# A build-time time model lets its DMAs land half a microsecond later

## The chip, the cores and the metric

The kernel runs on one core of one Trainium2 chip. The metric is the device time of one execution in microseconds (us). One first execution of 3502.34 us enters no ratio. Times of the same kernel differ a little from chip to chip.

## The reference

It is one adaLN transformer block: 2048 tokens of width 512, 32 heads of width 16, and a gated FFN of width 1792, all in bf16.

```python
mod = (_silu(c) @ w_mod)                      # six vectors of 512: sa, ca, ga, sb, cb, gb
h = _layernorm(x) * (1 + ca) + sa
x = x + ga * (softmax(q @ k.T / 4) @ v) @ wo  # q, k, v = heads of h @ wqkv
h = _layernorm(x) * (1 + cb) + sb
x = x + gb * (_gelu(h @ w_gate) * (h @ w_up)) @ w_down
```

The 32 x 2048 x 2048 exponentials set the pace: ScalarE computes most of them.

## The kernel before

The kernel is a program that writes a program. While it is built, a greedy loop decides at each step what each engine gets next. It asks a time model when an instruction's inputs will be there, and issues nothing that the model holds for not ready. The order that comes out is fixed. On the chip each engine follows its own order, and semaphores hold an instruction until its inputs really are there. So the model's error has a price: if it believes that data land earlier than they do, an engine stands still in front of an instruction with other work queued behind it.

The model of a DMA, in nanoseconds, with the constants it uses:

```python
LAND = 800
RATE = 175
...
    def model(self, op, t, cost):
        eng = op.eng
        if op.stream not in COMPUTE:
            self.free[eng] = t + 460
            early = t < 20000                       # the prologue
            self.dma_free = max(t + 1400, self.dma_free) + cost / (350 if early else RATE)
            op.t1 = self.dma_free + (1500 if early else LAND)
```

The DMAs shown here are those after each unit of attention (8 head groups for each set of query columns; 38 units pass here). Their denominators travel through DRAM, so that the reciprocal is taken 128 partitions wide and then comes back as a broadcast; the second of two units also moves the first one's neighbour rows inside `osb`:

```python
self.copy("dve", osb, acc[:, 0:W])                     # unit_end
self.dma("sp", s1..., self.osb[DH:P:32, lo:hi], "da")  # scr_den <- osb
# ... then as tasks, each issued when the model says its input is there:
self.dma("sp", den, s1..., "db")                       # den <- scr_den
self.recip(rden, den)                                  # VectorE
self.dma("sp", s2..., rden, "dc")                      # scr_rec <- rden
rd(j)    # j = 0..3:  rb <- scr_rec, broadcast to 16 partitions
move(j)  # j = 0..3, second unit only:  osb <- osb, from one 16 partitions to the next
fin2     # onorm <- osb * rb                           # VectorE; the output projection needs it
```

The other part is the "quads". Where the loop finds VectorE free enough by the model, it takes four 512-column score tiles away from ScalarE and computes their exponentials by integer arithmetic on VectorE and GpSimd.

The softmax here doesn't subtract the row's maximum and nothing guards it: scores larger than these inputs give would overflow.

Of the kernel before, what the change touches and what calls it, by code (L numbers as in the profile page):

```python
# [45 lines left out]
NS = 4  # L46
AHEAD = 20
PREFER = 300
LAND = 800
RATE = 175  # L50
POW = (350, 145)
SPACE = 12
# [54 lines left out]
class _Recorder:  # L107
# [181 lines left out]
# [4 lines that stand above are left out]
            early = t < 20000  # L293
            self.dma_free = max(t + 1400, self.dma_free) + cost / (350 if early else RATE)
            op.t1 = self.dma_free + (1500 if early else LAND)
        elif eng == "pe":
# [1456 lines left out]
```

## Time and profile before

| | before |
|---|---|
| median time | 813.48 us (the earlier three runs: 814.04) |
| span of the profiled run | 812.1 us |
| ScalarE busy | 775.7 us |
| ScalarE idle from 25 us to its last exponential | 7.24 us |
| from there to the end ("the tail") | 25.75 us |
| quads | 106 |
| VectorE's waits for den and rb | 9.5 us |

To read it: the last exponential is where ScalarE next loads another activation table (786.35 us here). Two stretches of the table of stretches, cut at that point, give the next two rows. Their columns are first and last us, length, then busy time (instructions) of PE (TensorE), PEld (its weight loads), DVE (VectorE), ACT (ScalarE) and POOL (GpSimd), the granted TensorE clock, the DMA share and GB/s:

```profile
25.00:786.35 761.35, 713.59 (x11725) 243.58 (x11724) 650.80 (x1161) 754.11 (x696) 244.33 (x139) 1.00 0.14 37
786.35:812.10 25.75, 21.85 (x284) 16.90 (x284) 12.11 (x24) 7.13 (x13) 0.80 (x2) 1.00 0.04 11
```

The idle time is 761.35 - 754.11 = 7.24 us. The quads are counted as the prediction does it, and the waits are its rows of rden for den and onorm for rb (8.1 + 1.4).

### The profile page before, as it was taken

To read this page: it belongs to the slowest core of one execution; us is meant where nothing else is said; L and a number is where in the kernel's file an instruction comes from. 1 tells how busy PE (TensorE), PEld (TensorE's weight loads), DVE (VectorE), ACT (ScalarE), POOL (GpSimd) and SP (SyncE) were. 2 spreads that over 40 slices of the span, in tenths; PEclk is the share of its full clock that TensorE was granted. 3 is DMA by queue.
4 is the path that set the end of the run, shared out by engine and by line. 5 is a ranking of instruction groups with operands and counts; after the bars stand their busy time and mean duration, and the time that the engine had idled before them with its cause. 6 is when DMAs were issued, how large, how long until landed. Compare 5 with 4: busy or idle time off the path is not lost.

```text
span 812.1 us, 27576 instructions
## 1 busy us (share of the span) xinstructions
PE 755.9 (93%) x12330; PEld 269.8 (33%) x12330; DVE 680.5 (84%) x1236; ACT 775.7 (96%) x729; POOL 252.4 (31%) x157
## 2 busy tenths in 40 slices
PE   8999999999989899899999998989989899998998
PEld 3333332322222222222222222222434333445466
DVE  6878988987898989898889899988688885697673
ACT  4999999999999999999999999999999899998972
POOL 2101426354465153346335351456130000010020
PEclk9999999999999999999999999999999999999999
DMA  9100000000022121111113111211232221120000
GB/s 313 52 9 12 15 10 15 10 17 10 16 64 62 31 53 48 35 41 29 29 37 94 30 47 45 61 29 29 54 91 57 58 68 39 36 71 11 17 14 14
DMA packets 58616, 36.03 MB, mean 44 GB/s; under 512 B 17961, under 2 KB 55074, under 8 KB 58498
## 3 DMA queue, kind: packets, MB, share of 16 engines
q1 hardware_dynamic: 56114, 32.71, 14.5%
q8 instruction: 96, 1.57, 0.8%
q10 hardware_dynamic: 2384, 1.57, 0.7%
q14 instruction: 22, 0.18, 0.1%
HBM read 29.62 MB, written 2.61 MB: 40 GB/s over the span
## 4 chain that ended last, share of the span: by engine, by line
ACT 69%; PE 19%; DVE 7%; DMA 3%; SPq 1%; issue 1%; POOL 0%; POOLq 0%; DVEq 0%
ACT E L379 66%; PE ps_mi L366 8%; PE ps_sc L366 7%; PE ps_pv L366 4%; ACT wreg L379 2%; DVE mreg L391 1%; DMA den<-scr_den 1%; SPq L430 1%; DVE wreg L400 1%; DMA mreg<-in_w_mod_dram 1%; DVE wreg L396 1%; DVE dreg L391 1%; DVE wreg L383 1%; DVE osb L400 0%; DMA scr_rec<-rden 0%
## 5 line engine op out<-in xcount | busy, mean ns | idle before, releaser
L379 ACT ACTIVATE E<-ps_sc 128x1024 bf16<-128x1024 f32 (+1 forms) x682 | 746.7, 1279 | 19.1 <-PE ps_sc L366 17.5
L391 POOL TENSOR_SCALAR mreg<-dreg 128x2048 uint16<-128x2048 uint16 x92 | 173.1, 1897 | 271.3 <-DVE mreg L391 130.8
L391 DVE TENSOR_SCALAR dreg<-ps_sc 128x512 uint16<-128x512 f32 x247 | 168.1, 687 | 36.1 <-PE ps_sc L366 34.9
L366 PE MATMUL ps_sc<-qT,kme 32*128 32x512 bf16 (+2 forms) x1318 | 172.9, 332 | 12.2 <-ACT E L379 10.2
L366 PE MATMUL ps_sc<-qT,kmo 32*128 32x512 bf16 (+2 forms) x1301 | 170.1, 332 | 6.7 <-ACT E L379 5.3
L366 PE MATMUL ps_pv<-E,vaug 128*17 128x512 bf16 (+2 forms) x2112 | 148.9, 328 | 1.0 <-DVE vaug L400 0.8
L366 PE MATMUL ps_pv<-mreg,vaug 128*17 128x512 bf16 (+2 forms) x1712 | 123.8, 339 | 1.8 <-DVE mreg L391 0.8
L366 PE MATMUL ps_mi<-wreg,mreg 128*32 128x512 bf16 (+1 forms) x1280 | 91.9, 374 | 7.5 <-DVE wreg L400 3.5
L391 POOL TENSOR_SCALAR mreg<-mreg 128x2048 uint16<-128x2048 uint16 x34 | 64.1, 1898 | 106.7 <-DVE mreg L391 57.2
L391 DVE TENSOR_SCALAR mreg<-ps_sc 128x512 uint16<-128x512 f32 x122 | 82.5, 686 | 11.1 <-PE ps_sc L366 9.9
L366 PEld LDWEIGHTS ps_sc<-qT,kme 32*128 32x128 bf16 x1318 | 46.1, 91 | 135.5 <-ACT E L379 108.0
L366 PEld LDWEIGHTS ps_sc<-qT,kmo 32*128 32x128 bf16 x1301 | 44.8, 91 | 127.6 <-ACT E L379 97.5
L391 DVE TENSOR_SCALAR mreg<-dreg 128x2048 uint16<-128x2048 uint16 x118 | 78.7, 686 | 1.5 <-PE ps_pv L366 1.4
L366 PEld LDWEIGHTS ps_pv<-E,vaug 128*17 128x17 bf16 x2112 | 44.0, 89 | 58.5 <-issue 47.3
L366 PEld LDWEIGHTS ps_pv<-mreg,vaug 128*17 128x17 bf16 x1712 | 38.3, 89 | 43.6 <-issue 18.1
L391 DVE TENSOR_SCALAR mreg<-mreg 128x2048 uint16<-128x2048 uint16 x74 | 49.1, 687 | 2.2 <-PE ps_pv L366 2.1
L643 POOL TENSOR_SCALAR mv<-mv 128x4 f32<-128x4 f32 (+2 forms) x10 | 2.3, 231 | 137.0 <-DVE mv L423 129.1
L366 PEld LDWEIGHTS ps_mi<-wreg,mreg 128*32 128x32 bf16 x1280 | 26.5, 95 | 46.4 <-issue 18.4
L366 PE MATMUL ps_mi<-hreg,wreg 128*32 128x512 bf16 x480 | 40.2, 384 | 0.2
L366 PE MATMUL ps_sc<-xs,ident 128*32 128x512 bf16 (+1 forms) x349 | 28.0, 388 | 13.2 <-ACT E L379 12.4
L400 DVE CAST wreg<-ps_mi 128x512 bf16<-128x512 f32 x49 | 33.6, 686 | 6.9 <-PE ps_mi L366 6.4
L396 DVE SCALAR_TENSOR_TENSOR wreg<-wreg,ps_mi 128x512 bf16<-128x512 bf16 x49 | 33.4, 682 | 5.8 <-PE ps_mi L366 3.8
(151 smaller groups left out, 704.8 us busy)
## 6 DMA issues: line engine op xcount, KB each, us to landing
mreg<-in_B_w_up_dram SPq DMA_DIRECT2D x22, 256.0 KB, 3.0
mreg<-in_B_w_gate_dram SPq DMA_DIRECT2D x15, 256.0 KB, 2.9
rb<-scr_rec SPq DMA_DIRECT2D x96, 32.0 KB, 1.8
dreg<-in_B_w_down_dram SPq DMA_DIRECT2D x9, 256.0 KB, 2.8
mreg<-in_w_mod_dram SPq DMA_DIRECT2D x1, 2048.0 KB, 14.6
mreg<-in_B_w_down_dram SPq DMA_DIRECT2D x8, 256.0 KB, 2.7
out_dram<-xs SPq DMA_DIRECT2D x16, 128.0 KB, 1.8
osb<-osb SPq DMA_DIRECT2D x48, 32.0 KB, 1.9
```

The costliest lines, as they stand in the source:

```text
L366: return self.rec("pe", lambda e: e.matmul(out, lhsT, rhs, start=start, stop=stop, tile_position=tp), [lhsT, rhs], [out], cost=(n, int(rhs ...
L379: return self.rec("act", lambda e: e.activation(out, in_, func, scale=scale, **kw), rd, wr, cost=self.cost("act", out, [in_], "act"))
L383: return self.rec(eng, lambda e: e.tensor_tensor(out, a, b, op), [a, b], [out], cost=self.cost(eng, out, [a, b], "tt"))
L391: return self.rec(eng, lambda e: e.tensor_scalar(out, a, s1, s2, **kw), rd, [out], cost=self.cost(eng, out, [a], "ts"))
L396: return self.rec("dve", lambda e: e.scalar_tensor_tensor(out, a, s, b, op0=op0, op1=op1), rd, [out], cost=self.cost("dve", out, [a, b], " ...
L400: return self.rec(eng, lambda e: e.tensor_copy(out, in_), [in_], [out], cost=self.cost(eng, out, [in_], "ts"))
L430: return e.dma_start(out, in_)
L643: self.rec("pool", lambda e: e.tensor_scalar(v, v, EPS, None, op0=ALU.add), [v], [v], cost=200)
```

## The change

```diff
-LAND = 800
+LAND = 1300
```

Nothing else. The model's landing outside the prologue moves by 500 ns, with the intent that readers of DMA'd data stand further back in their engines' order, behind work that can be done meanwhile.

## The prediction

> **What bounds the kernel now.** I read the page first (busy time, slices, chain that ended last), then the waits, the table of stretches, and the timeline of DVE and of the DMA queue around the longest DMA waits.
>
> ```profile
> PE 755.9 (93%) x12330; PEld 269.8 (33%) x12330; DVE 680.5 (84%) x1236; ACT 775.7 (96%) x729; POOL 252.4 (31%) x157
> ...
> ACT  4999999999999999999999999999999899998972
> ...
> ACT 69%; PE 19%; DVE 7%; DMA 3%; SPq 1%; issue 1%; POOL 0%; POOLq 0%; DVEq 0%
> ```
>
> ScalarE (ACT), which computes the exponentials, is busy for 775.7 of 812.1 us and carries 69% of the chain. Its idle time is 36.4 us. The table of stretches (first to last us, length, then busy time and count of PE, PEld, DVE, ACT, POOL, clock, DMA share, GB/s) says where:
>
> ```profile
> 0.00:25.00 25.00, 20.43 (x326) 9.33 (x330) 17.54 (x52) 14.45 (x21) 7.27 (x16) 0.93 0.90 295
> ...
> 300.00:400.00 100.00, 93.60 (x1224) 26.04 (x1220) 89.34 (x148) 100.00 (x96) 40.92 (x23) 1.00 0.14 37
> ...
> 600.00:640.00 40.00, 35.48 (x677) 13.84 (x680) 33.24 (x64) 37.68 (x33) 7.03 (x5) 0.96 0.24 66
> ...
> 720.00:760.00 40.00, 35.78 (x854) 18.63 (x850) 31.86 (x68) 37.27 (x36) 5.66 (x3) 0.96 0.06 12
> ...
> 785.00:812.00 27.00, 22.54 (x306) 17.23 (x302) 13.07 (x27) 8.47 (x15) 0.80 (x2) 1.00 0.03 11
> ```
>
> The start loses 25.0 - 14.45 = 10.55 us and the tail 27.0 - 8.47 = 18.53 us. Everything between, 25 to 785 us, loses 36.4 - 29.1 = 7.3 us, nearly all after 600 (2.3 in 600 to 640, 2.7 in 720 to 760). From 100 to 600 us ACT is full.
>
> ACT's work is not fixed. DVE and POOL take some score tiles ("quads" of four 512-column tiles) by an approximation. The groups give 247 + 122 + 33 + 22 = 424 tiles read from PSUM by DVE at L391, so 106 quads; the shifts agree (92 + 34 on POOL, 118 + 74 on DVE: 318 = 3 x 106). ACT has the rest: 276 activations of three tiles (395.5 us) and 398 of two (391.1 us), 1624 tiles, 786.6 / 1624 = 0.484 us a tile. **One quad more or fewer is worth 4 x 0.484 = 1.94 us of ACT.**
>
> Who waits for DMAs, apart from the DMA queue itself, in the waits (total us, times, longest):
>
> ```profile
> DVE rden L403 <- DMA den<-scr_den: 8.1, 10, 2.2
> ...
> DVE onorm L383 <- DMA rb<-scr_rec: 1.4, 1, 1.4
> ```
>
> After the prologue that is all that matters: no wait of a matmul for a weight load stands among the large ones. DVE's waits are the reciprocal of the softmax denominators and one normalisation. The worst one in the timeline, of DVE and then of the queue that issues the DMAs (SPq):
>
> ```profile
> 737.34 0.42 DVE L383 TENSOR_TENSOR wreg<-wreg 128x512 bf16<-128x512 bf16 x1
> 739.95 0.20 DVE L403 RECIPROCAL rden<-den 128x8 f32<-128x8 f32 x1 [2.19 <-DMA den<-scr_den]
> ...
> 732.98 0.54 SPq L430 DMA_DIRECT2D scr_den<-osb  x1
> 733.57 3.24 SPq L430 DMA_DIRECT2D osb<-osb  x4
> 736.85 0.58 SPq L430 DMA_DIRECT2D den<-scr_den  x1
> 740.18 0.34 SPq L430 DMA_DIRECT2D scr_rec<-rden  x1
> 741.61 1.71 SPq L430 DMA_DIRECT2D rb<-scr_rec  x4
> ```
>
> The path is scr_den, den, reciprocal, scr_rec, rb. Here four moves of osb stood between the first two hops, and from the first issue to the reciprocal 6.97 us went by.
>
> **What the Trainium skill says.** "DMA: Bandwidth & Descriptors", section "Rules for kernel authors", advises to issue a DMA early, compute, and wait late: that is what the change asks of the order. Its section "Two DMAs through the same engine are not ordered" says that a DMA that reads what another wrote must wait for its semaphore, so each hop of the path pays a whole latency; the trace agrees: the DMA queue waits 34.6 us for scr_rec and 16.8 us for scr_den. Its section "Anatomy of one DMA" (for the path issued by GpSimd) gives about 2.0 us fixed; this trace, on SP's path, has medians of 1.8 us to landing for the 8 KB den loads and 2.9 us for 256 KB of weights. "Perfetto Trace Analysis", section "DMA Instruction — HWDGE (DVE, Sync)", says that the reported window ends when the sequencer is free and leaves the data's movement out; agreed: den's row is 0.58 us, its reader starts 3.10 us after the row begins.
>
> **The change, part by part.** It removes and adds no instruction by itself. LAND is a constant of the model by which the program orders its own instructions while it is built; on the chip the semaphores decide. After 20 us of model time a DMA lands at issue + 1400 ns + bytes / 175 + LAND. An 8 KB hop: 1400 + 47 + 800 = 2.25 us, after the change 2.75. 256 KB: 1400 + 1498 + 800 = 3.70 us, after 4.20. Both were already above the medians of 1.8 and 2.9 us; only hops behind other DMAs are slower (3.1 us above, up to 3.9).
>
> (a) Reciprocals. Two hops lie before each of the 38, so it stands about 1.0 us further back. The model's first two hops become 5.5 us instead of 4.5, against 6.97 in the worst case. Of the ten waits (0.3, 0.8, 0.3, 1.1, 0.6, four making 2.8, and 2.2 us) about 1.0 each goes: some 6.5 of the 8.1 us. The onorm wait of 1.4 us, four hops back (2.0 us), goes too. But DVE is not the bound: only what reached ACT counts. Near 485 us ACT lost at most 0.6 us in its whole 100 us; near 670 us none; at 741.7 ACT idled 1.72 us for a DVE product that followed the 2.19 us wait; at 637 to 638 us it idled 1.82 + 0.50 us for scores soon after the onorm wait at 632. The upper end is 0.6 + 1.7 + 1.4 = 3.7 us; I count half, **-1.8 us**.
>
> (b) Later normalisations. A unit of attention (38 of them) is normalised four hops after its end, so 2.0 us later in the model. The output projection and all of the FFN of the set follow it. Before 600 us this is slack: units end about every 20 us, the buffers come free some 11 to 13 us after an end. At the two places where the side work is tight, after the sets that end near 600 and near 730 us, and at the last normalisation (778.2 us, needed by the projection at 780.96, so 2 us of slack), part of 2 us comes back each time. An estimate of half: 3 x 1 x 0.5 = **+1.5 us**.
>
> (c) Weights. Streamed pieces are double buffered, reader and load some 8 us apart in the paced stretch, so 0.5 us is hidden; **0**.
>
> (d) The order as a whole. Every decision is greedy and depends on model times, so it all changes from the first DMA after 20 us on. What decides is how many quads are started. A later model landing makes side work look idle for longer (then quads are allowed freely: more), and moves normalisations back into the time in which DVE takes quads (fewer). I cannot derive the sign. 2 quads either way are 3.9 us; tail alignment is a few us more. The constants look tuned around 800, so I add **+1.8 us** for a disturbed optimum; that is a judgement and no measurement.
>
> Sum: 814.0 - 1.8 + 1.5 + 0 + 1.8 = **815.5 us**.
>
> **The rivals.**
> 1. The model was too optimistic where moves crowd the queue, the waits go, and the time falls by the 3.7 us of (a) or, with more quads, by more: 806 to 811 us. For it: ten waits at the same reciprocal, 6.97 us real against 4.5 modelled. Against: ACT is full for 500 us and idles only 7.3 us between start and tail, so without more quads even a perfect order stays above 806.
> 2. The landing was already pessimistic (1.8 and 2.9 us against 2.25 and 3.70), so readers that were ready stand behind others, side work starts later and the tail grows: each set's 2 us comes through, the side work piles up at the end where PE's ps_mi products lead the chain, and two or three quads are lost: 820 to 828 us. For it: after 600 us the chain is mostly PE and DVE side work. Against: 18.5 us of tail hold no DMA that anything but the end waits for.
> 3. Nothing: ACT's full stretch hides all of it and the two effects cancel, 812 to 816 us.
>
> **Range and chances.** Rival 3 and the middle of 1 and 2 give 806 to 826 us for 8 in 10. A gain of 2% is 16.3 us: more than twice all of ACT's idle time outside start and tail, so it needs at least five quads more as well. A loss of 2% needs eight quads fewer, or a stall of the side work that the buffers cannot hide. Chances: faster 0.03, within 2% 0.90, slower 0.07.
>
> **What would show it.** Step (a) is right if the wait of rden for den falls from 8.1 to about 1.6 us, and the onorm wait goes. Step (b) is right if the onorm rows stand about 2 us later after their unit's osb copy. Step (c): no new wait of PE for wreg, mreg or dreg weight loads. Step (d): the count of L391 reads of PSUM (424) stays within 8; the ACT busy time moves by 1.94 us per quad; ACT's idle time from 25 to 785 us stays below 12 us. The prediction is wrong if the number of quads moves by five or more, or the tail after the last exponential, now 26 us, changes by more than 3 us.

## The result, and the profile after

The changed kernel took 809.41 us in the median of four runs (808.04 to 810.54) against 813.48 for the kernel before. The ratio is 0.9952 with a 95% interval of 0.9928 to 0.9977: half a per cent faster, and within 2%. A ratio here is the mean time of one kernel's runs over that of the other's runs of the same rounds, so not quite the ratio of the quoted medians.

From the page of the changed kernel: busy times, ScalarE's slices, and the chain that ended last.

```profile
PE 752.7 (93%) x12355; PEld 273.1 (34%) x12359; DVE 689.0 (85%) x1252; ACT 770.0 (95%) x733; POOL 262.3 (32%) x162
...
ACT  4999999999999999999999999999999999999961
...
ACT 83%; PE 12%; DVE 3%; DMA 2%; issue 0%; SPq 0%; DVEq 0%
```

ScalarE does 5.7 us less work, carries 83% of the chain in place of 69%, and runs empty earlier (the last two slices are 6 and 1 tenths instead of 7 and 2). The waits for DMAs in the trace of the changed kernel (total us, times, longest):

```profile
DVE onorm L383 <- DMA rb<-scr_rec: 1.4, 1, 1.4
DVE rden L403 <- DMA den<-scr_den: 1.4, 1, 1.4
```

The reciprocals waited 8.1 us before and wait 1.4 us now. The same cut of stretches (the last exponential is over at 777.03 us):

```profile
25.00:777.03 752.03, 707.41 (x11705) 245.07 (x11705) 658.26 (x1176) 749.16 (x702) 254.54 (x145) 1.00 0.14 38
777.03:808.20 31.17, 25.29 (x347) 19.23 (x340) 14.03 (x29) 7.12 (x13) 0.80 (x2) 0.93 0.04 14
```

| us of the span | before | after | difference |
|---|---|---|---|
| ScalarE idle, 25 us to last exponential | 7.24 | 2.87 | -4.37 |
| ScalarE busy in the same stretch | 754.11 | 749.16 | -4.95 |
| tail | 25.75 | 31.17 | +5.42 |
| span (the three rows and the first 25 us) | 812.1 | 808.2 | -3.90 |

The groups count 258 + 134 + 30 + 14 = 436 tiles by integer arithmetic, so 109 quads, three more: 3 x 1.94 = 5.8 us of ScalarE. But the tail took back 5.42 us, in part through the granted clock: its mean was 0.93 there, and 0.50 from 784 to 786 us. From the busy times and clocks of the stretches between 782 and 788 us, an estimate is that 1.4 us of TensorE's 25.29 come from this. So two stories fit the sum: the stalls went and the quads were given back, or the quads were the gain and something else grew the tail. The experiments decide between them.

### The profile page after: what moved, and what is told of

Same layout as the page of the kernel before. It is cut to its first block, busy times and chain, and to the rows that moved or that the text cites. A ratio compares the mean times of both kernels' runs of the same rounds, so it can differ in the third digit from the quotient of the medians.

```text
span 808.2 us, 27649 instructions
## 1 busy us (share of the span) xinstructions
PE 752.7 (93%) x12355; PEld 273.1 (34%) x12359; DVE 689.0 (85%) x1252; ACT 770.0 (95%) x733; POOL 262.3 (32%) x162
## 4 chain that ended last, share of the span: by engine, by line
ACT 83%; PE 12%; DVE 3%; DMA 2%; issue 0%; SPq 0%; DVEq 0%
ACT E L379 80%; PE ps_sc L366 6%; PE ps_mi L366 3%; ACT wreg L379 3%; PE ps_pv L366 2%; DMA mreg<-in_w_mod_dram 1%; DVE mreg L391 1%; DMA den<-scr_den 1%; DMA rb<-scr_rec 0%; DVE wreg L383 0%; DVE dreg L391 0%; SPq L430 0%; DVE wreg L391 0%; DVE xs L383 0%; PE ps_sc L370 0%
## 5 line engine op out<-in xcount | busy, mean ns | idle before, releaser
L379 ACT ACTIVATE E<-ps_sc 128x1024 bf16<-128x1024 f32 (+2 forms) x686 | 742.5, 1265 | 15.6 <-PE ps_sc L366 14.5
L391 POOL TENSOR_SCALAR mreg<-dreg 128x2048 uint16<-128x2048 uint16 x93 | 175.2, 1898 | 271.1 <-DVE mreg L391 114.0
L391 DVE TENSOR_SCALAR dreg<-ps_sc 128x512 uint16<-128x512 f32 x258 | 175.0, 687 | 32.0 <-PE ps_sc L366 30.2
L366 PE MATMUL ps_sc<-qT,kmo 32*128 32x512 bf16 (+2 forms) x1316 | 173.5, 332 | 10.7 <-ACT E L379 9.6
L391 DVE TENSOR_SCALAR mreg<-ps_sc 128x512 uint16<-128x512 f32 x134 | 91.1, 686 | 15.3 <-PE ps_sc L366 14.8
L391 POOL TENSOR_SCALAR mreg<-mreg 128x2048 uint16<-128x2048 uint16 x38 | 71.6, 1898 | 96.1 <-PE ps_sc L366 48.7
L391 DVE TENSOR_SCALAR mreg<-dreg 128x2048 uint16<-128x2048 uint16 x123 | 81.2, 687 | 0.5 <-PE ps_pv L366 0.4
L366 PEld LDWEIGHTS ps_pv<-mreg,vaug 128*17 128x17 bf16 x1768 | 40.4, 89 | 35.0 <-issue 10.9
L366 PE MATMUL ps_sc<-xs,ident 128*32 128x512 bf16 x353 | 28.7, 398 | 11.4 <-ACT E L379 11.2
```

The source lines that it names most:

```text
L366: return self.rec("pe", lambda e: e.matmul(out, lhsT, rhs, start=start, stop=stop, tile_position=tp), [lhsT, rhs], [out], cost=(n, int(rhs ...
L379: return self.rec("act", lambda e: e.activation(out, in_, func, scale=scale, **kw), rd, wr, cost=self.cost("act", out, [in_], "act"))
L391: return self.rec(eng, lambda e: e.tensor_scalar(out, a, s1, s2, **kw), rd, [out], cost=self.cost(eng, out, [a], "ts"))
```

## The experiments

**Theory W:** the loss was the waits for DMAs, and the gain is that they went. **Rival Q:** the gain is the other greedy order with its three more quads; the waits were hidden by a full ScalarE. For the tail, **theory G** (the extra quads' gain is given back there) stands against **rival H** (the quads are the gain).

Where an order is kept and single instructions are moved, the order of the greedy pass was taken as a list, edited, and all dependences and semaphores were worked out anew. With an empty edit this gave the unchanged program. "Modelled end" is the end of the kernel's own time model after the build; with 800 and with 1300 it is the same, 798.2 and 798.1 us. So the model, which believes its own landings, sees no gain in the changed order.

One question needed no run. With 1300 for the five kinds of denominator DMA alone (da, db, dc, dd and the moves) the build gave the changed program, instruction for instruction. With 1300 for all others but these, only the order of a few DMAs on the issuing queue changed. So the whole effect of the change comes through the denominators.

### First group: moving the readers, and the opposite constant

In `rec_later` and `both_later` the readers are moved inside the order of before, in `both_sooner` inside the order of after (a move stops early where a dependence forbids it):

```diff
+ for i in reciprocals(order):     later(order, i, 1000)    # rec_later: 1000 ns of modelled VectorE work
+ for i in normalisations(order):  later(order, i, 1000)    # both_later: these first, then the reciprocals
+ ...                              sooner(order, i, 1000)   # both_sooner
```

`land600` sets the constant the other way:

```diff
-LAND = 800
+LAND = 600
```

> The order of the kernel before is kept, quads and all (106), and only the 38 reciprocals of the denominators are moved behind about 1.0 us more of DVE work each, with the DMAs that depend on them. Theory W (the waits for the DMAs were the loss, made larger by the TensorE clock that drops after the stall): the wait of the reciprocals for den falls from 8.1 us to under 2.5, the stall at 738 to 746 us with its granted clock of 0.50 is gone, ACT's idle time before the last exponential falls by about 2 us, time about 811.5. Theory Q (the gain is the three more quads and another greedy order, the waits were hidden): the wait falls all the same, but the time stays within 1 us of before, 813 to 814.

> As the run with the reciprocals moved, and the 19 normalisations that read the reciprocals' broadcast are moved back by about 1.0 us of DVE work too, as far as their readers allow. Theory W: the stall at 632 to 640 us (onorm for rb, 1.4 us, then granted clock 0.50) goes as well, ACT's idle time before the last exponential falls from 17.8 to about 14 us, time about 810, with 106 quads. Theory Q: 813 to 814.

> The order of the kernel after the change is kept, with its 109 quads, and the reciprocals and normalisations are moved forward by about 1.0 us of DVE work, which gives the waits back. Theory W: the wait of rden for den rises from 1.4 to about 8 us or more, one or two stalls with a low granted clock come back before the last exponential, and the time rises by 2 to 5 us over the kernel after, to 811 to 814. Theory Q: the waits rise and the time stays at 809 to 810.

> The constant is set to 600 instead of 800: the opposite direction. The program that comes out has 109 quads, three more than before, as the changed kernel has, but its readers stand nearer to their DMAs. Theory W: the reciprocals wait longer than 8.1 us, about 15, and most of the gain of the quads (5.8 us of ACT) is lost to stalls: no better than 811. Theory Q: as fast as the changed kernel or faster, 805 to 810.

(The 17.8 us of ScalarE's idle time that `both_later` names count the first 25 us too: 10.55 + 7.24. The tables below leave the start out.)

Measured, against 814.6 us for the kernel before on the same chip:

| run | quads | waits for den + rb, us | ScalarE idle to last exp. | tail | median us | ratio (95%) |
|---|---|---|---|---|---|---|
| rec_later | 106 | 1.0 + 11.8 | 7.70 | 25.94 | 817.33 | 1.0039 (1.0016 to 1.0062) |
| both_later | 106 | 1.3 + 1.1 | 7.81 | 25.76 | 812.63 | 0.9975 (0.9952 to 0.9997) |
| both_sooner | 109 | 14.6 + 3.1 | 11.89 | 31.78 | 821.74 | 1.0109 (1.0079 to 1.0140) |
| land600 | 109 | 11.7 + 3.6 | 8.30 | 27.10 | 811.95 | 0.9974 (0.9956 to 0.9992) |

`rec_later` is a miss of theory W as it was put, and of the 813 to 814 us of rival Q as well: the wait for den went, but the time rose. The waits of its VectorE show what happened to the wait.

```profile
DVE onorm L383 <- DMA rb<-scr_rec: 11.8, 9, 3.7
DVE rden L403 <- DMA den<-scr_den: 1.0, 1, 1.0
```

A later reciprocal starts the next two hops later, and the normalisations at their end had not been moved. The wait went one reader down the path and grew. What this cost is not shown: the profiled run is the fastest of the six (813.62 us against a median of 817.33), and its span, 811.9 us, is that of before.

`both_later` gains a quarter per cent, half of what was expected, although both waits are nearly gone. Its profiled run, the slowest of its six (813.92 us), shows a new stall that the edit made itself: a moved normalisation stood in front of the projection that TensorE needed next, and waited for its own later DMA. The rows of VectorE, of TensorE and of the table of stretches around it:

```profile
593.86 0.69 DVE L383 TENSOR_TENSOR onorm<-osb,rb 128x512 bf16<-128x512 f32 x1 [1.13 <-DMA rb<-scr_rec]
...
594.61 0.62 PE L366 MATMUL ps_mi<-wo,onorm 128*32 128x512 bf16 x4 [2.65 <-DVE onorm L383]
...
594.00:596.00 2.00, 1.39 (x18) 0.41 (x18) 1.27 (x3) 0.00 (x0) 0.00 (x0) 0.50 0.64 176
596.00:598.00 2.00, 2.00 (x25) 0.55 (x26) 1.36 (x3) 1.76 (x2) 0.00 (x0) 0.50 0.33 91
```

This shows what a wait can do. VectorE waits 1.13 us, TensorE behind it is idle for 2.65 us, then the granted clock is 0.50 (in all the stretches from 594 to 600 us), and ScalarE loses 3.8 us for want of scores. Readers pushed back by hand, with the rest left where it is, are no clean test; the greedy pass plans around them and this edit does not.

`both_sooner` is the opposite: the changed order, 109 quads, with the readers moved forward. The waits come back (17.7 us) and the time is 1.1% above before, more than the 811 to 814 us that were expected. `land600` has the same number of quads as the changed kernel and a modelled end of 793.8 us, the best of all, but 15.3 us of waits; it gains a quarter per cent where theory Q expected 805 to 810 us. Both speak for W, but both change more than the waits.

### Second group: the readers stay, the DMAs land sooner

The clean test leaves the order of the four compute engines alone and takes away what delays the landing. The prediction's timeline shows four moves of 16 partitions inside `osb` between the first two hops. `no_moves` leaves out all 76; the result is wrong (the check of results passes it all the same). Every instruction of TensorE, VectorE, ScalarE and GpSimd is the same as before, in the same order.

```diff
+ order = [i for i in order if not is_move(i)]   # no_moves on the order before, no_moves_after on the changed one
```

`moves_priced` is the constructive version: a right result, LAND back at 800, and a model that knows the moves. The 620 ns of the queue are what the trace shows (four moves in 2.46 us); where the 650 and the 1200 come from is not on record. The 1200 holds for every DMA, not for the moves alone.

```diff
-            self.free[eng] = t + 460
             early = t < 20000
-            self.dma_free = max(t + 1400, self.dma_free) + cost / (350 if early else RATE)
+            move = op.stream[2:4] == "mv" and not early
+            self.free[eng] = t + (620 if move else 460)
+            self.dma_free = max(t + (1400 if early else 1200), self.dma_free) + (650 if move else cost / (350 if early else RATE))
```

> The changed kernel once more, as a control on the chip of the next three runs. Both theories: a ratio of 0.993 to 0.998 to the kernel before, as in its own rounds (0.9952).

> The kernel before with its 76 moves inside osb (two stretches of 16 partitions, four for each pair of units) left out; the result is wrong on purpose, and the order of TensorE, VectorE, ScalarE and GpSimd is the same, instruction for instruction. The loads of den and rb then have the queue to themselves. Theory W (waits for DMAs were the loss): the wait for den falls from 8.1 us to under 3, both stalls with a granted clock of 0.50 go, ACT's idle time before the last exponential falls by 3 to 4 us, the time by about 3.5, to a ratio of about 0.9955, with 106 quads and no change of order at all. Theory Q (quads and order): ratio 0.999 to 1.001.

> The changed kernel with its moves left out in the same way; wrong result on purpose. Theory W: the changed kernel has 2.8 us of DMA waits left and hardly any on the path, so it gains at most 1 us, ratio to the kernel before 0.994 to 0.996; and it lies within 1.5 us of the kernel before without moves, since the time model puts the ends of the two orders at the same time (798.2 and 798.1). Theory Q: it gains nothing and stays about 4 us ahead of the kernel before without moves.

> The constant stays at 800, and the time model is told instead what the trace shows of the moves: 620 ns of the issuing queue and 650 ns of the DMA engines for each, and a start of transfer 1200 ns after the issue for all DMAs in place of 1400. An order with 108 quads comes out, with a modelled end of 794.5 against 798.2. Theory W: waits for den and rb together under 4 us, and as the model is then near the truth, a time of 804 to 808, better than both kernels. Theory Q: the same sign from the quads alone, about 810.

Measured, against 815.62 us for the kernel before on the same chip:

| run | quads | waits for den + rb, us | ScalarE idle to last exp. | tail | median us | ratio (95%) |
|---|---|---|---|---|---|---|
| after_again | 109 | 1.0 + 1.3 | 2.40 | 31.34 | 808.04 | 0.9917 (0.9896 to 0.9938) |
| no_moves | 106 | 1.4 + 0 | 1.81 | 25.80 | 808.01 | 0.9900 (0.9882 to 0.9918) |
| no_moves_after | 109 | 0 + 1.0 | 2.32 | 31.69 | 807.53 | 0.9896 (0.9877 to 0.9915) |
| moves_priced | 108 | 1.8 + 0.8 | 1.13 | 25.50 | 803.67 | 0.9854 (0.9836 to 0.9873) |

`after_again`, the control, fell just outside its 0.993 to 0.998: on this chip the change is worth 0.8%. `no_moves` decides. With the same order and 106 quads it is as fast as the changed kernel, and its gain of 1% is twice what theory W expected. That the moves held up some other transfer is no way out: between 25 and 790 us of the kernel before, the waits of VectorE for den and rb are the only ones for a DMA that the view of the waits lists for any compute engine. Its denominator load and the scr_rec store after it, in the DMA queue, answer to the rows around 737 us of the kernel before:

```profile
730.65 0.50 SPq L430 DMA_DIRECT2D scr_den<-osb  x1
732.26 0.34 SPq L430 DMA_DIRECT2D den<-scr_den  x1
735.57 0.34 SPq L430 DMA_DIRECT2D scr_rec<-rden  x1
...
735.35 0.20 DVE L403 RECIPROCAL rden<-den 128x8 f32<-128x8 f32 x1
```

Before, 6.97 us went by from the first issue to the reciprocal; here the reciprocal stands at 735.35, 4.70 us after it, without a wait. What that wait had done to TensorE and ScalarE is in TensorE's row and the stretches, first of the kernel before:

```profile
740.96 0.51 PE L366 MATMUL ps_mi<-wreg,qT 128*32 128x256 bf16 x12 [1.83 <-DVE wreg L396]
...
738.00:740.00 2.00, 1.13 (x34) 0.60 (x30) 0.05 (x1) 2.00 (x2) 0.00 (x0) 1.00 0.05 6
740.00:742.00 2.00, 1.04 (x22) 0.46 (x26) 1.67 (x5) 0.28 (x2) 0.00 (x0) 0.88 0.04 2
742.00:744.00 2.00, 2.00 (x36) 0.88 (x35) 0.78 (x2) 1.99 (x3) 0.00 (x0) 0.50 0.09 28
```

and then of the kernel without moves, at the same place in the program:

```profile
735.00:737.00 2.00, 2.00 (x70) 1.37 (x58) 1.96 (x7) 2.00 (x2) 0.00 (x0) 1.00 0.07 10
737.00:739.00 2.00, 2.00 (x60) 1.07 (x56) 1.04 (x3) 2.00 (x3) 0.00 (x0) 1.00 0.02 7
```

Before, VectorE stands (0.05 us busy of 2), TensorE is half idle for 4 us, the clock falls to 0.50, and ScalarE is busy for 0.28 us of 2. Without moves none of it happens. The same picture stands before at 632 to 640 us (clock 0.50 from 636 to 638), behind the onorm wait. The Trainium skill's page "TensorE: Matmul & The Clock Gate", section "HAM oscillation — how this bites in real kernels", says that idle gaps of more than about 3.4 us put TensorE's clock back to 4/8. The half clock fits (0.50), but here one gap of 1.83 us, as the trace gives it before the matmuls at 740.96, with a half-idle stretch around it was enough. That the drop of the clock enlarges the loss is read from these stretches; no run held the clock up through such a wait.

Nor does the clock follow the DMA waits alone. In the changed kernel it fell at 272 us, with no DMA wait near and no gap of TensorE above 0.62 us in the four us before, and ScalarE then lost 1.15 of its 2.87 us; at 446.96 us a reciprocal waited 1.37 us, TensorE stood for 0.24 us at most, and the clock stayed up. The stretches of the changed kernel from 270 us:

```profile
270.00:272.00 2.00, 1.38 (x24) 0.53 (x24) 2.00 (x5) 2.00 (x3) 0.00 (x0) 0.90 0.00 0
272.00:274.00 2.00, 2.00 (x23) 0.54 (x15) 1.02 (x2) 2.00 (x2) 1.42 (x1) 0.50 0.00 0
```

`no_moves_after` gains nothing certain over the changed kernel (the intervals overlap), and it lies on `no_moves`: 0.9896 and 0.9900. (Both are faster than the 0.994 to 0.996 that was expected.) Without the waits the two orders are equally fast, as the model has them, and in this order the three quads are worth nothing. Rival Q is out.

`moves_priced` is 1.5% faster than the kernel before and, by the two ratios (0.9854 / 0.9917), 0.6% faster than the changed one on the same chip, with a right result: it has few waits, 108 quads, and the short tail. Which of these is worth how much, this run alone does not show.

### Third group: the quads and the tail

`cap106` and `cap108` are the changed kernel with a limit on the quads, so all is the same until the last ones would start. `long_tail` is `moves_priced` with other constants, and `no_moves_600` is `land600` without its moves (wrong).

```diff
-                    elif (cand and self.quad_free and ...
+                    elif (cand and nquad < 106 and self.quad_free and ...      # or 108
+                        nquad += 1
```

```diff
-LAND = 800                                # long_tail, beside the edit of moves_priced
+LAND = 850
-    max(t + (1400 if early else 1200), ...
+    max(t + (1400 if early else 1300), ...
```

> The changed kernel with the number of quads held at 106, as before the change: the last three are not started, and everything up to them is the same. Theory G (the three extra quads gave nothing in the end, since TensorE's side work then falls into the tail): the last exponential ends about 5 us later than in the changed kernel (777.0), the tail after it shrinks from 31 to about 26 us, and the time equals that of the changed kernel within 2 us, a ratio of 0.990 to 0.995 to the kernel before. Rival H (the quads are the gain): it loses 5.8 us and is back at a ratio of 0.998 to 1.002.

> The changed kernel without its last quad, 108. Theory G: the last quad costs more in the tail than it saves ScalarE; the modelled end is 795.7 against 798.1 with 109 and 797.9 with 106, so about 2 us faster than the changed kernel, a ratio of 0.988 to 0.992. Rival H: 1.9 us slower than the changed kernel.

> The model with the moves priced as in the run moves_priced, but with 50 ns more of landing and 100 ns more before each transfer: again 108 quads and a modelled last exponential 0.6 us earlier (771.0 against 771.6), yet a modelled end of 804.0 against 794.5. Theory G: quads and DMA waits are the same (under 4 us), ScalarE's last exponential at about 776, and the whole difference lies in the tail: 33 to 36 us in place of 25.5, so 811 to 814 against 803.7. Rival H: as fast as moves_priced, since ScalarE has the same work and no waits.

> The order of the run land600 (109 quads) with the moves inside osb left out; wrong result on purpose. Theory W: land600 lost its quads to 15.3 us of DMA waits; without the moves most of them go, and the time comes near what the model promises for it (794.5 or so to the kernel before's 798.2, which took 808.0 without moves): 803 to 806, a ratio of 0.985 to 0.989. Theory Q: as land600, a ratio of 0.996 to 0.998.

Measured, against 813.93 us for the kernel before on the same chip:

| run | quads | modelled end | waits for den + rb, us | ScalarE idle to last exp. | tail | median us | ratio (95%) |
|---|---|---|---|---|---|---|---|
| cap106 | 106 | 797.9 | 1.0 + 1.0 | 2.09 | 25.47 | 805.83 | 0.9895 (0.9878 to 0.9912) |
| cap108 | 108 | 795.7 | 3.6 + 2.0 | 1.45 | 26.92 | 804.70 | 0.9880 (0.9865 to 0.9896) |
| long_tail | 108 | 804.0 | 3.3 + 1.3 | 1.66 | 36.08 | 814.93 | 1.0004 (0.9984 to 1.0023) |
| no_moves_600 | 109 | 793.8 | 1.0 + 2.7 | 3.92 | 27.11 | 803.80 | 0.9872 (0.9856 to 0.9889) |

With 106 quads the changed order keeps the whole gain (its ratio is no higher than the 0.9952 and 0.9917 of the changed kernel, which was timed on other chips). The last exponential is over at 780.23 us, 3.2 us later than with 109, and the tail is 5.7 us shorter, in the table of stretches of `cap106`:

```profile
25.00:780.23 755.23, 710.00 (x11675) 244.57 (x11673) 648.16 (x1161) 753.14 (x702) 250.68 (x142) 1.00 0.14 38
780.23:805.70 25.47, 21.11 (x274) 16.73 (x279) 11.84 (x23) 7.13 (x13) 0.81 (x2) 1.00 0.04 12
```

So rival H, which expected 0.998 to 1.002, is out: the three quads did not pay. That the last of them cost time (`cap108`) is likely but not shown, since the changed kernel was not timed on this chip. `long_tail` shows the same from the other side. It has the quads of `moves_priced`, few waits and nearly the same last exponential (776.82 against 775.90 us), and is as slow as the kernel before, because of its tail, which makes 10.58 of the 11.5 us between the two spans:

```profile
776.82:812.90 36.08, 29.24 (x378) 21.14 (x369) 16.84 (x34) 7.24 (x13) 1.61 (x4) 0.95 0.05 16
```

TensorE works 29.24 us in that tail, against 21.85 us in the tail of before and 25.29 us in that of after (by the same estimate as above, 1.6 us of the 29.24 come from a clock of 0.50 to 0.90 between 788 and 794 us). The FFN of the last sets is TensorE's work, and a ScalarE that finishes early does not make it shorter. The FFN of the fourth of the six sets ends with two output tiles. The product that finishes the second one starts at 769.70 us before and at 781.08 us after, 4 us behind the last exponential; the rows of the two timelines, before and then after:

```profile
769.70 0.68 DVE L383 TENSOR_TENSOR wreg<-ps_mi,gb 128x512 bf16<-128x512 f32 x1
```

```profile
781.08 0.69 DVE L383 TENSOR_TENSOR wreg<-ps_mi,gb 128x512 bf16<-128x512 f32 x1
```

`no_moves_600` closes the account of `land600`: by the two ratios (0.9872 / 0.9974) it is 1% faster without its moves than with them, and it comes to 803.8 us, as theory W expected.

The modelled ends say the same once more. In the runs with at most 5.6 us of waits, the changed kernel among them, the median lies 7.9 to 11.3 us above the modelled end; it lies 15.3 to 17.4 us above it for the kernel before, and 18.2 us for `land600` (`rec_later`, `both_later` and `both_sooner` apart, whose orders the model did not plan). So the model's order of the kernels is right to some 3 us, apart from the waits that it does not see.

## Why the prediction was right

**The sum.** It said 815.5 us in a range of 806 to 826 and a 90% chance of within 2%; measured were 809.41 us and within 2%. The direction of the middle was wrong: it leaned 1.5 us to slower, and the kernel is 4.1 us faster in the medians. Of the rivals the first was nearest, "the waits go, and the time falls by the 3.7 us of (a)".

**Step (a), reciprocals: mechanism right, size too small.** The waits of rden fell from 8.1 to 1.4 us where 1.6 was forecast. The delay from a unit's osb copy to its reciprocal, averaged over the 38 units in the timelines, rose from 6.6 to 7.9 us, by 1.3 for the 1.0 forecast. The term was -1.8 us with an upper end of 3.7; ScalarE's idle time fell by 4.37 us, and by 5.43 us (7.24 to 1.81) where the moves alone were taken away. The upper end, 0.6 + 1.7 + 1.4, was meant to be ScalarE's idle time near the waits, but its last piece is VectorE's own wait, where ScalarE lost the 1.82 + 0.50 us that the working names itself. And it missed what followed the stall at 740 us: with the granted clock at 0.50, ScalarE ran short three times more, 0.30 + 0.40 + 0.29 us by 750 us. With these the sum is 5.6. Halving the sum for caution made it worse.

**Step (a), onorm.** The stall at 632 us went, but another of 1.4 us came, at 770.10 us, close to the tail.

**Step (b), later normalisations: right in kind, and free.** From the second unit's osb copy to the normalisation the mean rose from 14.3 (11.9 to 18.1; the working reads 11 to 13 for the buffers) to 17.1 us, 2.8 where 2.0 was forecast. The +1.5 us charged for it did not show: with the quads held at 106 the tail was 25.47 us, as short as before.

**Step (c), weights: right.** The landing of weights has no effect on any compute engine's order, and after 25 us the changed kernel's waits list none of TensorE for a load.

**Step (d), the order as a whole: the term that failed.** "I add +1.8 us for a disturbed optimum" had nothing under it: the model's end was the same for both orders, and the chip puts them level too once the waits are gone (`no_moves` and `no_moves_after`). The quads moved by three, beyond the "two either way" and its check of 8 tiles (12 moved). The tail grew by 5.4 us, beyond the 3 us that the prediction had named as a sign of being wrong. These two cancelled, so the total stayed inside the range partly by luck. The working had priced a quad at 1.94 us of ScalarE without asking whether TensorE, 93% busy and owing the FFN, could follow.

## What to carry to other kernels

If a program orders itself by a time model, compare the model's landing with the trace for each place where an engine waits, and correct the term that is wrong there. A constant added to every DMA does it too, but it delays readers that were never late; here pricing the moves, with every transfer's start set 200 ns earlier, gave 1.5% where the constant gave 0.5 to 0.8%. That is no proof that the better model gives the better order: `long_tail` prices the moves the same way, differs from `moves_priced` by 150 ns in all, and has no gain. A greedy order can change a lot with a small constant, so compare the modelled ends of several before choosing one. And time taken off the bounding engine counts only as far as the engine that owns the tail can follow: look at who works after the bound has finished before crediting the saving.

## What the Trainium skill lacked or had wrong

- "DMA: Bandwidth & Descriptors" (section "Issuing engines are not separate DMA queues") calls the sequencer's time to initiate a DMA usually small relative to the DMA itself. Here a move of 16 partitions inside SBUF took 0.59 us of the issuing queue in the median (a den load 0.52) against 1.9 and 2.6 us to landing, and four in a row held the queue for 3.24 us (2.46 us at other places), longer than the 1.8 us in which a den load lands.
- The same page has no figure for a small load issued behind such moves. Its reader started 3.10 us after the issue of den, where the median landing of den loads was 1.8 us.
- "TensorE: Matmul & The Clock Gate" (section "HAM oscillation — how this bites in real kernels") puts the harmful idle gap at more than about 3.4 us. In these runs gaps of 1.83 and 2.65 us, and once several of at most 0.62 us, in stretches where TensorE was otherwise partly busy, were followed by a granted clock of 0.50. (Elsewhere the page tells of clock drops from frequent short idles, but gives no length for them.)
- No page has a figure for what a wait of an in-order engine costs the engine behind it: with the order kept, taking away 8.1 of the 9.5 us of VectorE's DMA waits gave back 5.4 us of ScalarE's idle time.
